# A fused attention and feed-forward kernel: its instructions issued in the main block of the program instead of in a block of their own

## The chip, the cores and the metric

The kernel runs on one core of a Trainium2 chip. The metric is the device time of one execution in microseconds (us), as the median over several runs. A core has five engines with an instruction stream each: TensorE (PE in the profile; its weight loads are PEld), VectorE (DVE), ScalarE (ACT), GpSimd (POOL) and SyncE (SP). They meet only over semaphores.

## The reference

The kernel computes attention in a sliding window of 32 positions to either side, for 8 batches of 8 heads, 576 positions and a head size of 64, and feeds the result, as 4608 tokens of 512 numbers, through two matrix products with a squared ReLU between them.

```python
scores = scale * np.matmul(q, k.transpose(0, 1, 3, 2))
mask = np.abs(pos[:, None] - pos[None, :]) <= window
scores = np.where(mask, scores, -1000000000.0)
...
attn = attn / (np.sum(attn, axis=-1, keepdims=True) + 1e-09)
out = np.matmul(attn, v)
...
h = x @ w_in            # (4608, 512) @ (512, 2048)
r = np.maximum(h, 0.0)
g = r * r
return (g @ w_out)      # (4608, 2048) @ (2048, 512)
```

## The kernel before

The attention goes through 24 groups of 192 queries (`NG`), three for each batch. For each group q and k are loaded, turned so that the head size lies on the partitions, multiplied (`scores`), put through the exponential and the mask, multiplied with v (`pv`), divided by the row sums and turned once more into `XT` (`xturn`). The feed-forward part follows some groups behind: `mm1` multiplies a stretch of `XT` with the first weights and squares the ReLU into `GT`, and `mm2` multiplies 128 tokens of `GT` with the second weights and stores 128 rows of the output. The last 128 tokens are cut into three pieces of columns (`mm2_last`, lines 766 to 779), so that eviction and store of the first pieces lie beside the matmuls of the later ones. ScalarE issues the stores of the first and third piece, SyncE that of the second.

No engine function issues instructions directly. Each step calls `rec`, which notes the engine, the function to call, what it reads and writes, an estimated duration and a key. `Prog.schedule` then simulates the engines and the DMA queues with these durations and sorts all operations by their planned start. `Prog.emit` goes through that one list, issues for each operation the waits that it needs (line 248) and then the operation itself, on its engine's queue.

The end of `Gen.build` is where this is put together. After `p.schedule()` a block of the language is entered (line 859), `p.emit()` issues every instruction of the kernel, and seven waits are issued on SyncE (line 863), one for each semaphore of the output stores (`o0` to `o3`, `oA`, `oB`, `oC`). Pairs of these waits are joined, so that four instructions of the trace carry line 863. Then the block is left, and what it issues on being left has line 859 in the trace. No body for a single engine is opened in the block; the engines are addressed as `nc.tensor`, `nc.scalar` and so on. Line 884 constructs the program object, before the kernel is called, and what the constructor issues has that line.

Of the kernel before, what the change touches and what calls it, by code (L numbers as in the profile page):

```python
# [270 lines left out]
class Gen:  # L271
# [511 lines left out]
    def build(self):  # L783
        p = self.p
        self.k1 = 0
        self.moe = None
        K = -100.0
        self.setup_idle()
        self.setup_iota(K + IOTA)
        self.setup_id(K)  # L790
        self.setup_mask(2, K + 1)
        self.setup_bias(2, K + 1.1)
        self.setup_mask(1, K + 2)
        self.setup_bias(1, K + 2.1)
        self.setup_k(0, K + 0.5)
        self.setup_v(0, K + 1.5)
        self.setup_v(1, VSET[0])
        self.setup_v(2, VSET[1])
        self.setup_mask(0, MKEY[0])
        self.setup_mask(3, MKEY[1])  # L800
        for i in range(3, NV):
            self.setup_v(i, -9)
        self.setup_k(1, -9)
        for n, it in enumerate(self.opening()):
            kd, a = it[0], it[1:]
            key = K + n
            if kd == "w1":
                self.load_w1(a[0], key)
            elif kd == "w2":
                self.load_w2(a[0], key)  # L810
            elif kd == "v":
                self.load_v(*divmod(a[0], 3), key, a[1:])
            elif kd[0] == "h":
                self.load_hw(kd[1], a[0], key)
            else:
                self.load_pair(kd, *divmod(a[0], 3), key)
        for g in (1, 2, 4, 5):
            self.copy_v(g, K + 7 if g < 3 else 3 * g - LEAD - AHEAD)
        todo = []

        def at(key, f, *a):
            todo.append((key, len(todo), f, a))

        for G in range(NG):
            b, g = divmod(G, 3)
            if b > 1:
                key = 3 * G - LEAD - AHEAD
                for t in "kq":
                    for c in PIECES[t][g]:
                        at(key, self.load_qk, t, b, c, key)  # L830
                at(key, self.load_v, b, g, key)
                if g and G < NVR:
                    key = 3 * G - LEAD - 0.5 if G >= VCS else key
                    at(key + 0.01, self.copy_v, G, key - VKEY if G >= VCS else key)
            for t in "kq":
                key = 3 * G - LEAD - (0.6 if b < NTURN else 3)
                for c in (g,) if b < NTURN else PIECES[t][g]:
                    at(key, self.turn_pe if b < NTURN else self.turn_dma, t, b, c, key)
            for ws in ((0,), (1,)) if G < NSPLIT else ((0, 1),):
                at(3 * G - LEAD + 0.3 * ws[0], self.scores, G, ws)  # L840
            for w in range(2):
                at(3 * G - LEAD + 0.3 * w + 0.1, self.pv, G, w)
            at(3 * G - LEAD + 0.5, self.xturn, G)
        t0 = 0
        while t0 < NTOK:
            n = FIRST[t0] if t0 in FIRST else 192 if t0 < 768 else 256 if t0 < T512 else 512
            m = min(512 // n, 4)
            for d in range(0, 16, m):
                key = t0 / 64 + d / 16 * n / 64
                at(key, self.mm1, t0, n, list(range(d, d + m)), key)  # L850
            t0 += n
        at(500, self.mm2_last, NBLK - 1, 500)
        for u in range(NBLK - 1):
            for seg in range(4):
                at(2 * u + LAG + seg * 0.5, self.mm2, u, seg, 2 * u + LAG + seg * 0.5)
        for key, _, f, a in sorted(todo, key=lambda x: x[:2]):
            f(*a)
        p.schedule()
        with self.nc.Block():
            dsems, dcount = p.emit()  # L860
            for s in dsems:
                if s[0] == "o":
                    self.nc.sync.wait_ge(dsems[s], dcount[s])
# [35 lines left out]
```

## Time and profile before

| what | before |
|---|---|
| time, median of 3 runs | 303.6 us |
| lowest and highest run | 303.34 and 303.64 us |
| span of the profiled execution, first to last instruction | 301.1 us |
| TensorE busy in the span | 291.9 us (97%) |
| instructions in the trace | 6232 |
| mean granted TensorE clock | 1.000 |

The profile is of one execution. Its span goes from the first to the last instruction of the program; the page shows no time of that execution beside the span, and the median of the runs is the nearest to it. Drains, waits and other instructions of an engine's sequencer are in the trace, with a small q behind the engine's name, but don't count as busy time. Views of one line list its instructions with the number of them, the least, median and longest duration in ns, and the first and last start in us from the span's start. The chain of waits is followed back from the last instruction that an engine, and not its sequencer, executed.

### The profile page before, as it was taken

The page shows a single profiled execution, that of the slowest core. Times are in us where ns is not written, and L with a number is a line of the kernel's source. Part 1 is how long each engine was busy: PE and PEld are TensorE (multiplying, and loading weights), DVE is VectorE, ACT ScalarE, POOL GpSimd, SP SyncE. Part 2 cuts the span into 40 slices and gives each one's busy share as a digit, 9 for nine tenths or more (in the row PEclk, how much of TensorE's full clock was granted, in tenths as well). Part 3 has the DMA queues.
Part 4 walks back from the last instruction along what each step waited for, and adds up shares of the span by engine and source line. Part 5 has one row for each costly group of instructions (what it writes and reads, how often), then busy time and mean ns, then how long its engine had stood idle before and what let it go on. Part 6 is the DMA issues. An engine that isn't in the chain of part 4 may idle for free.

```text
span 301.1 us, 6232 instructions
## 1 busy us (share of the span) xinstructions
PE 291.9 (97%) x2394; PEld 170.9 (57%) x2431; DVE 166.5 (55%) x385; ACT 160.7 (53%) x250; POOL 102.4 (34%) x131
## 2 busy tenths in 40 slices
PE   7899999999999999999999999999999999999996
PEld 2578866846677777764444445445444444444445
DVE  5898785726766766664378756666456322222100
ACT  3587834826567646644656666455636443443312
POOL 8993335406543543654065454330000000000000
PEclk9999999999999999999999999999999999999999
DMA  9999999999998999999999999994121201000112
GB/s 167 176 206 183 196 178 176 168 163 208 175 158 138 141 160 191 147 157 177 199 152 135 166 162 143 199 168 101 54 50 49 60 35 37 35 35 36 37 70 105
DMA packets 160060, 39.83 MB, mean 132 GB/s; under 512 B 149408, under 2 KB 155552, under 8 KB 160032
## 3 DMA queue, kind: packets, MB, share of 16 engines
q0 software_dynamic: 105824, 17.93, 86.1%
q1 hardware_dynamic: 48880, 12.14, 28.4%
q10 hardware_dynamic: 5328, 9.37, 8.9%
q8 instruction: 19, 0.31, 0.4%
q14 instruction: 9, 0.07, 0.1%
HBM read 36.70 MB, written 9.44 MB: 153 GB/s over the span
## 4 chain that ended last, share of the span: by engine, by line
PE 87%; DMA 7%; POOL 3%; issue 1%; ACT 1%; DVE 0%; ACTq 0%; POOLq 0%
PE ht L721 41%; PE outp L741 38%; DMA w<-in_moe_w_in_dram 5%; PE at L606 4%; PE at L548 3%; DMA xt<-xa 2%; POOL v L427 1%; POOL w L440 1%; PE at L469 1%; PE ht L766 1%; PE outp L766 1%; POOL kpair L410 1%; POOL qpair L410 1%; ACT rt L727 0%; ACT oe L751 0%
## 5 line engine op out<-in xcount | busy, mean ns | idle before, releaser
L721 PE MATMUL ht<-xt,w 128*128 128x256 bf16 (+2 forms) x886 | 142.4, 302 | 1.7 <-DMA xt<-xa 0.5
L741 PE MATMUL outp<-w,gt 128*128 128x512 bf16 x535 | 134.3, 379 | 1.4 <-issue 0.2
L727 ACT ACTIVATE rt<-ht 128x512 bf16<-128x512 f32 (+1 forms) x152 | 86.4, 577 | 90.8 <-PE ht L721 85.7
L721 PEld LDWEIGHTS ht<-xt,w 128*128 128x128 bf16 x896 | 80.8, 98 | 43.8 <-DMA xt<-xa 1.0
L730 DVE TENSOR_TENSOR gt<-rt 128x512 bf16<-128x512 bf16 (+1 forms) x152 | 61.3, 408 | 65.0 <-ACT rt L727 63.2
L741 PEld LDWEIGHTS outp<-w,gt 128*128 128x128 bf16 x560 | 52.3, 98 | 56.0 <-ACT oe L751 1.1
L378 POOL DMA_DIRECT2D kraw<-in_k_dram x30 | 25.3, 850 | 95.2 <-PE at L548 76.5
L573 ACT ACTIVATE e<-at 128x1024 bf16<-128x1024 f32 x46 | 44.8, 1021 | 11.2 <-PE at L548 11.1
L578 DVE TENSOR_TENSOR pt<-e,mask 128x1024 bf16<-128x1024 bf16 x46 | 31.5, 691 | 24.7 <-ACT e L573 24.6
L427 POOL DMA_DIRECT2D v<-in_v_dram x48 | 38.4, 822 | 0.0
L751 ACT ACTIVATE oe<-outp 128x512 f32<-128x512 f32 x35 | 21.1, 602 | 24.1 <-PE outp L741 24.1
L378 POOL DMA_DIRECT2D qraw<-in_q_dram x30 | 25.5, 860 | 0.0
L606 PEld LDWEIGHTS at<-v,pt 128*128 128x128 bf16 x384 | 18.0, 98 | 10.0 <-DVE at L634 1.8
L606 PE MATMUL at<-v,pt 128*128 128x65 bf16 x384 | 20.1, 194 | 0.5 <-ACT pt L570 0.5
L628 DVE TENSOR_TENSOR xb<-at,rs 128x512 bf16<-128x512 f32 x24 | 16.6, 690 | 1.1
L628 DVE TENSOR_TENSOR xa<-at,rs 64x512 bf16<-64x512 f32 x24 | 16.7, 695 | 0.8
L548 PEld LDWEIGHTS at<-qt,kt 64*128 64x128 bf16 x384 | 10.8, 94 | 8.3 <-issue 7.5
L548 PE MATMUL at<-qt,kt 64*128 64x128 bf16 x384 | 15.2, 217 | 0.1
L625 DVE RECIPROCAL rs<-at 64x8 f32<-64x8 f32 (+1 forms) x48 | 10.0, 209 | 9.5 <-PE at L606 7.8
L634 DVE MEMSET at<- 64x520 f32 x23 | 11.3, 492 | 3.7 <-DVE xa L628 2.9
L434 DVE COPY v<-v 64x512 bf16<-64x512 bf16 x16 | 5.8, 366 | 6.9 <-PE ht L721 5.8
L773 DVE COPY oe<-ht 128x128 f32<-128x128 f32 x1 | 0.3, 291 | 14.7 <-PE ht L766 14.7
(67 smaller groups left out, 82.1 us busy)
## 6 DMA issues: line engine op xcount, KB each, us to landing
out_dram<-oe ACTq DMA_DIRECT2D x35, 256.0 KB, 3.8
kraw<-in_k_dram POOLq DMA_DIRECT2D x24, 128.0 KB, 5.6
qraw<-in_q_dram POOLq DMA_DIRECT2D x24, 128.0 KB, 5.9
w<-in_moe_w_in_dram POOLq DMA_DIRECT2D x4, 512.0 KB, 10.6
v<-in_v_dram POOLq DMA_DIRECT2D x16, 128.0 KB, 7.3
w<-in_moe_w_out_dram POOLq DMA_DIRECT2D x4, 512.0 KB, 18.9
v<-in_v_dram POOLq DMA_DIRECT2D x16, 96.0 KB, 6.7
v<-in_v_dram POOLq DMA_DIRECT2D x16, 64.0 KB, 5.8
```

Source lines behind the costliest of these rows:

```text
L378: self.p.rec("POOL", lambda e: e.dma_start(raw[0:n, x % 2, :].rearrange("p (h d) -> p h d", h=8), s), writes=[("raw", t, x // 2, x % 2)], ...
L427: self.p.rec("POOL", lambda e, j=j, lo=lo, hi=hi, k0=k0: e.dma_start(vt[lo - k0:hi - k0, j, :, 0:64], self.v[b, :, lo:hi, :].rearrange("h ...
L548: mm = e.matmul(sc[:, 512 * par + 128 * j:512 * par + 128 * j + 128], kt[r:r + 64, j, k0:k0 + 128], q, start=G >= NBIAS, stop=True, skip_g ...
L573: self.p.rec("ACT", lambda e, e_=e_, sc=sc: e.activation(e_[:], sc, ACTF.Exp, scale=0.125), reads=tags[w], writes=[("e", n % 2)], key=key, ...
L578: self.p.rec("DVE", lambda e, pt=pt, ee=ee, mb=mb: e.tensor_tensor(pt[:], ee, mb, ALU.mult), reads=[("e", n % 2), ("mask", mi)], writes=[( ...
L606: mm = e.matmul(avp[:, c:c + 65], pt[:, 4 * (h % 2) + h // 2, :], vt[:, w, h, 0:65], start=(w == 0 and y == 0), stop=True, skip_group_chec ...
L628: self.p.rec("DVE", lambda e: e.tensor_tensor(x[r0:128, :].rearrange("p (x y c) -> p x y c", x=2, y=4), av[:, :, :, 0:64], rb, ALU.mult), ...
L721: mm = e.matmul(ht[:, n * x:n * x + n], self.W1[:, ft, 128 * d:128 * d + 128], self.XT[:, ft, r:r + n], start=(ft == 0), stop=(ft == 3))
L727: self.p.rec("ACT", lambda e: e.activation(rt[:, 0:c], ht[:, 0:c], ACTF.Relu), reads=[f"ht{k % 2}"], writes=[("rt", k % 4)], key=key, dur= ...
L730: self.p.rec("DVE", lambda e: e.tensor_tensor(gt[:, d0:d0 + len(ds), r:r + n], rr, rr, ALU.mult), reads=[("rt", k % 4)], writes=[("gt", s, ...
L741: mm = e.matmul(op[:], gt[:, d, r:r + 128], self.W2[:, d, :], start=(d == 0), stop=(d == 15))
L751: self.p.rec("ACT", lambda e: e.activation(oe, op[:], ACTF.Copy), reads=[f"outp{u % 2}"], writes=[("oe", u % 4)], key=key, dur=act(512), n ...
```

## The change

The block is no longer entered. `p.emit()` and the waits for the stores stand under a condition that is always true, with the same indentation, so that they are issued in the block that is open when the kernel is called, the program's main block. Nothing else of the kernel is different.

```diff
@@ -856,7 +856,7 @@
         for key, _, f, a in sorted(todo, key=lambda x: x[:2]):
             f(*a)
         p.schedule()
-        with self.nc.Block():
+        if True:
             dsems, dcount = p.emit()
             for s in dsems:
                 if s[0] == "o":
```

## The prediction

> **What bounds the kernel now.** I read the page of the profiled execution first, then the view of everything issued from the line of the block, the waits of SyncE, and the first and last microseconds. The page:
>
> ```profile
> span 301.1 us, 6232 instructions
> PE 291.9 (97%) x2394; PEld 170.9 (57%) x2431; DVE 166.5 (55%) x385; ACT 160.7 (53%) x250; POOL 102.4 (34%) x131
> ...
> PE 87%; DMA 7%; POOL 3%; issue 1%; ACT 1%; DVE 0%; ACTq 0%; POOLq 0%
> ```
>
> TensorE is busy for 97% of the span and makes up 87% of the chain of waits. A change that leaves the order and the waits of the matmuls alone can touch only what lies ahead of the first matmul, behind the last one, or outside the span. So the two ends are what has to be read. The last microseconds, in the order of time:
>
> ```profile
> 297.82 0.94 PE L766 MATMUL ht<-w,gt 128*128 128x128 bf16 x14
> 297.92 0.29 DVE L773 COPY oe<-ht 128x128 f32<-128x128 f32 x1 [14.66 <-PE ht L766]
> ...
> 298.23 0.38 SPq L779 DMA_DIRECT2D out_dram<-oe  x1
> 298.87 0.28 ACT L776 ACTIVATE oe<-ht 128x128 f32<-128x128 f32 x1 [1.46 <-PE ht L766]
> 299.18 0.34 ACTq L779 DMA_DIRECT2D out_dram<-oe  x1
> ```
>
> Behind the last matmul (297.82 + 0.94 = 298.76) come one eviction on ScalarE and the last store, issued at 299.18. Its transfer takes this long, and SyncE waits for it at line 863:
>
> ```profile
> DMA to landing us min/median/max: 1.6/1.7/1.7
> ...
> L863 SPq EVENT_SEMAPHORE  x4: 17/28/28, 298.7 to 300.8; - x4
> ```
>
> 299.18 + 1.7 is 300.9, and the last of SyncE's four waits stands at 300.8, so it is the landing of the last store that ends it. The span ends at 301.1. The rest is what the block issues when it is closed:
>
> ```profile
> L859 POOLq EVENT_SEMAPHORE  x2: 17/17/17, 300.9 to 301.0; - x2
> L859 POOLq DRAIN  x1: 7294/7294/7294, 197.2 to 197.2; - x1
> L859 PEldq DRAIN  x1: 1195/1195/1195, 297.6 to 297.6; - x1
> L859 DVEq DRAIN  x1: 328/328/328, 297.9 to 297.9; - x1
> L859 ACTq DRAIN  x1: 153/153/153, 299.6 to 299.6; - x1
> L859 SPq DRAIN  x1: 13/13/13, 300.9 to 300.9; - x1
> L859 SPq EVENT_SEMAPHORE  x1: 17/17/17, 301.1 to 301.1; - x1
> L859 ACTq EVENT_SEMAPHORE  x1: 17/17/17, 301.1 to 301.1; - x1
> L859 DVEq EVENT_SEMAPHORE  x1: 21/21/21, 301.1 to 301.1; - x1
> L859 PEldq EVENT_SEMAPHORE  x1: 51/51/51, 301.1 to 301.1; - x1
> ```
>
> These are all the instructions that line 859 has in the trace: five drains and six semaphore instructions, 11 in all, with first start 197.2 and last start 301.1. Not one of them stands at the beginning, and none is a branch. It is a barrier: each engine drains and reports, GpSimd collects the reports and releases the others, and each passes when released. Entering the block costs nothing here; only closing it does.
>
> **The change, part by part.** *What stays at the beginning.* There is a barrier of the same make in the first microsecond, from line 884, which constructs the program object, and which the diff doesn't touch:
>
> ```profile
> L884 POOLq EVENT_SEMAPHORE  x2: 17/17/17, 0.5 to 0.6; - x2
> L884 SPq DRAIN  x1: 7/7/7, 0.0 to 0.0; - x1
> ...
> L884 PEldq EVENT_SEMAPHORE  x1: 51/51/51, 0.7 to 0.7; - x1
> ```
>
> The first transfers, matmuls and weight loads start behind that one, and go on starting behind it. Nothing at the front is removed, added or moved: 0.
>
> *What stays in the middle.* The work of all queues is sorted by the planner before the block is entered, and each instruction is issued in that order with its own waits, with or without a block. The block opens no body for a single engine. So SyncE's loads and transposes, GpSimd's loads and ScalarE's stores keep their places: 0, and if I am wrong here, TensorE's 291.9 us will say so.
>
> *What goes at the end.* The four drains of GpSimd, TensorE, VectorE and ScalarE lie beside other work. The longest, GpSimd's 7.294 us, begins at 197.2 and is over at 204.5, some 96 us ahead of the end. TensorE's is over at 297.6 + 1.2 = 298.8, VectorE's at 297.9 + 0.3 = 298.2, ScalarE's at 299.6 + 0.15 = 299.75. All lie under the flight of the last store, which lands at 300.8. Removing them gains nothing; without that cover they would cost up to 1.2 us (TensorE's). What is not covered is all that follows SyncE's last wait: its drain of 13 ns, the collecting and releasing on GpSimd (2 x 17 ns and the ways between), and the passing of the released engines, TensorE's 51 ns as the longest. SyncE's own time in it has a row, the only wait of line 859 there:
>
> ```profile
> SPq L863 <- DMA out_dram<-oe: 2.0, 3, 0.8
> SPq L859 <- PEq L859: 0.2, 1, 0.2
> ```
>
> So the uncovered part is 0.013 + 0.2 + 0.051 = 0.26 us. The rounding of the two ends bounds it: the last wait ends between 300.78 and 300.88 (300.75 to 300.85, and 28 ns), and the span between 301.05 and 301.15, which leaves 0.17 to 0.37. For the collecting half there is the barrier at the beginning, in the chain of waits:
>
> ```profile
> 0.56 0.06 issue
> 0.62 0.02 POOLq L884
> 0.64 0.11 issue
> 0.75 0.01 POOLq L316
> ```
>
> From 0.56 to 0.75 it is 0.19 us, without a drain before it and the 51 ns behind it; together 0.25. I take 0.26.
>
> *What takes its place.* Nothing of the kernel's own is late next: SyncE's four waits for the stores stay, so the program still ends with the last landing. Four engines now run off the end of their streams early, by rows above at 204.5 or before (GpSimd), 298.2, 298.8 and 299.75, instead of all at 301.1. What the chip does with them then has no row: the trace holds the kernel's instructions alone. The page gives no time for the profiled execution beside its span. The runs' median of 303.6 is 2.5 us above the span, and these 2.5 us hold everything ahead of the first and behind the last instruction, profiling differences included. So the unknown term is bounded by -2.5 (all of it is done early) and, on the other side, by the dearest drain of an engine that still has work, +1.2 less the 0.26. Of its values I take 0: SyncE, the engine that is last in both kernels, still has its whole way through the ending ahead of it.
>
> The sum: 301.1 - 0.26 = 300.84 for the span, and 303.6 - 0.26 = 303.34 for the time, or 303.3.
>
> There is one page that bears on the unknown term: in the Trainium skill, "Runtime: NRT & Kernel Launch", section "The ~15µs preamble/postamble breakdown" says that after the kernel the runtime places a barrier of its own in which all engines are waited for, and that clearing the semaphores comes only behind it. By that rule the early engines can't begin the ending, so the gain stays at the barrier's own time, 0.26; its figures for that ending, about 1.5 us for the barrier and about 1.5 for the clearing, add to more than the 2.5 us that lie outside the span here, and the rule's order is not visible in this trace.
>
> **The rivals.** *The ending shrinks too.* If each engine has something of its own to do at the end of a program before it meets the others, four of five now do it under the flight of the last store, and only SyncE's part is left. For it: GpSimd, VectorE, TensorE and ScalarE are free at least 1.0 us before 300.8. Against it: SyncE is last as before, and if the parts are done side by side and are of one length, the gain is nil. The price: take half of the 2.5 us as lying behind the span, 1.25, and half of that as saved, 0.6. Then 303.34 - 0.6 = 302.7.
>
> *The barrier is hidden anyway.* Another meeting of the engines follows at once, and the one that goes had already lined them up; its time is then spent in the next one. For it: the barrier at the beginning takes the same 0.25 us, so engines that have to be lined up pay about this whoever asks for it. Against it: a second meeting needs its own time behind the first one, so both are in the time of before. Time 303.6.
>
> *Slower: the emptying of the engines comes at the end.* The drains stand now where they cost nothing, each behind its engine's last work. If an engine is instead emptied by what follows the program, and only after SyncE's last wait, a drain comes onto the path. It decides when it exceeds the 0.26 us that went. For it: GpSimd's drain took 7.294 us at its place and TensorE's 1.195, so they are not always short. Against it: both had work in flight when they began; SyncE's drain at 300.9, with nothing in flight, took 13 ns, and by 300.8 every engine is in that state. At TensorE's price the time is 303.34 + 1.2 = 304.5.
>
> *The change doesn't do what it says.* If a barrier is issued at the end of every program anyway, the 11 instructions come back under another line. For it: one is issued at the beginning without being asked for (line 884). Against it: that one belongs to the constructor. Time 303.6, as for the hidden barrier.
>
> **How the numbers follow.** Forecast 0.54 at 303.3, with a range of its own of 303.0 to 303.6, since the three runs of before lie 0.3 us apart (303.34 to 303.64); the shrinking ending 0.30 at 302.7; hidden anyway or not done, together 0.09 at 303.6; slower 0.07 at 304.5. The predicted time is the likeliest, 303.3. Down to 302.6 the range takes in more than half of the shrinking ending, and up to 303.7 all of the hidden barrier; what is left out is the rest of the one and the slower case, under 0.2. What a measurement can tell from no change is about 0.2%, 0.6 us: faster means below 303.0, slower above 304.2. The forecast puts 0.06 below 303.0 and the rest within; the shrinking ending 0.28 below and 0.02 within; the cases at 303.6 put 0.08 within and 0.01 above. That is 0.34 faster, 0.58 within, and 0.08 slower.
>
> **What would show it.** No drain and no semaphore instruction from line 859, and 6232 - 11 = 6221 instructions. The last instruction of the trace is SyncE's fourth wait at line 863, and the span is 300.8 to 300.9. Line 884 has the same rows, and TensorE is busy for 291.9 us within a few tenths. If the span falls by 0.26 but the time falls by more than 0.6, the ending shrinks. If the span falls and the time doesn't, the barrier was hidden. If TensorE's busy time or its first matmul moves by more than a few tenths, then the block did something to the stream that this trace doesn't show, and my reading of line 859 is wrong.

## The result, and the profile after

The changed kernel took 302.39 us (median of 10 runs, 301.48 to 303.15); the kernel before, run beside it and counted with its three earlier runs, took 303.3 us (10 runs, 303.06 to 304.06). The ratio is 0.9966, with a 95% interval of 0.9953 to 0.998: faster by 0.9 us. The prediction was 303.3, in a range of 302.6 to 303.7; the measured time lies below the range.

First the page of the changed kernel, then its view of what line 863 issues (instructions, least, median and longest ns, first and last start), then its answer for line 859:

```profile
span 301.5 us, 6221 instructions
...
PE 292.0 (97%) x2394; PEld 171.4 (57%) x2431; DVE 166.6 (55%) x385; ACT 160.7 (53%) x250; POOL 102.6 (34%) x131
```

```profile
L863 SPq EVENT_SEMAPHORE  x4: 17/28/28, 299.4 to 301.5; - x4
```

```profile
nothing on L859; most used: ['L721', 'L741', 'L548', 'L606', 'L248', 'L469', 'L727', 'L730', 'L766', 'L378', 'L509', 'L313', 'L427', 'L625', 'L628', 'L573', 'L578', 'L751', 'L753', 'L634', 'L701', 'L704', 'L884', 'L434', 'L597']
```

The 11 instructions are gone, TensorE is as busy as before, and the program ends with SyncE's last wait. So far it is as forecast. But this execution's span is longer than the one shown of before (301.5 against 301.1), though a barrier is missing from it, and its time is shorter. Each run of the changed kernel has its own time and span, and they answer the second half of this: 302.86 and 301.5, 301.48 and 300.2, 303.15 and 301.8. **Time less span** is 1.28 to 1.36 us in all ten, with a mean of 1.33. Before the change only one span was known, and no time of the same execution.

Where the span went is in the timelines of TensorE, before and after (start, duration, and in brackets the idle time before):

```profile
69.33 1.05 PE L721 MATMUL ht<-xt,w 128*128 128x256 bf16 x8 [0.53 <-DMA xt<-xa]
```

```profile
70.14 1.03 PE L721 MATMUL ht<-xt,w 128*128 128x256 bf16 x8 [1.12 <-issue]
```

These are the only waits of TensorE in its timelines between 60 and 90 us. The same matmul waited 0.6 us longer in the execution shown of after. What it waits for is a turned tile of the attention's result, which SyncE sends for with line 701; the profile names this releaser before, and none after ("issue"). The views of that one transfer, before and after, show that it was issued at about the same time and took 0.8 us longer to land, at about 69.2 and 70.1 us, each time just ahead of the matmul:

```profile
L701 SPq DMA_TRANSPOSE xt<-xa x1: 1267/1267/1267, 62.0 to 62.0; - x1
...
DMA to landing us min/median/max: 7.2/7.2/7.2
```

```profile
L701 SPq DMA_TRANSPOSE xt<-xa x1: 1272/1272/1272, 62.1 to 62.1; - x1
...
DMA to landing us min/median/max: 8.0/8.0/8.0
```

So this part of the difference lies 230 us ahead of the end of the program. The end itself:

```profile
299.54 0.28 ACT L776 ACTIVATE oe<-ht 128x128 f32<-128x128 f32 x1 [1.40 <-PE ht L766]
299.84 0.34 ACTq L779 DMA_DIRECT2D out_dram<-oe  x1
```

From the issue of the last store (299.84) to the end of the span it is 1.7 us; before it was 1.9 (299.18 to 301.1), so the barrier's quarter of a microsecond did go.

### The profile page after: what moved, and what is told of

It is laid out like the page before. It is cut to its first block, busy times and chain, and to the rows that moved or that the text cites. A ratio compares the mean times of both kernels' runs of the same rounds, so it can differ in the third digit from the quotient of the medians.

```text
span 301.5 us, 6221 instructions
## 1 busy us (share of the span) xinstructions
PE 292.0 (97%) x2394; PEld 171.4 (57%) x2431; DVE 166.6 (55%) x385; ACT 160.7 (53%) x250; POOL 102.6 (34%) x131
## 4 chain that ended last, share of the span: by engine, by line
PE 90%; DMA 5%; POOL 3%; issue 1%; ACT 1%; POOLq 0%; ACTq 0%
PE ht L721 41%; PE outp L741 40%; DMA w<-in_moe_w_in_dram 5%; PE at L606 4%; PE at L548 3%; POOL v L427 1%; POOL w L440 1%; PE at L469 1%; PE ht L766 1%; PE outp L766 1%; POOL kpair L410 1%; POOL qpair L410 1%; ACT rt L727 0%; ACT oe L751 0%; ACT oe L776 0%
```

## The experiments

Two views were held against each other. *Theory E*: the ending of the program, outside the span, got shorter, because it no longer begins on all engines at once. *Rivals*: the ending is the same, and only the wandering span made the difference (S); or the drains, and not the lateness of the engines, make the ending long (D). What tells them apart is time less span, taken run by run: it also holds what lies ahead of the first instruction, so only differences of it are read. Between runs of one kernel it varied by about 0.1 us, at most by 0.2, while times and spans wander by some 2 us and more. All kernels but the one that changes the slack run the same operations in the same order; the order of the waits of one operation is not fixed by the source, and spans are known to 0.1 us, so span differences below that are not read.

**The kernel before, unchanged.**

> The kernel before, unchanged, to have time and span of the same execution. Theory E (the ending shrinks): time less span is 2.2 to 2.5 us in every run, against the 1.33 us of the changed kernel, and the spans lie between 300.7 and 301.7. Rival S (the ending is the same and only the stream ran differently): time less span is 1.3 us here too, and the spans lie near 302.

Time less span was 2.15 us on average (2.11 to 2.18); over the runs of before beside it, 31 in number, 2.13. That is a little below what theory E expected (2.2 to 2.5) and far from S, which falls: against the changed kernel's 1.33, 0.80 of the gain lies outside the span.

**The changed kernel, built anew.**

> The changed kernel once more, built anew. Theory E: time less span is 1.28 to 1.36 us again, whatever the span. Rival S: the difference of 0.9 us to the kernel before doesn't come back; ratio 0.998 to 1.002.

302.3 us against 303.45, ratio 0.9953 (0.9933 to 0.9973), and time less span 1.32. The gain came back.

**The four other engines held until SyncE is done.** The edit, in the changed kernel:

```diff
-                    self.nc.sync.wait_ge(dsems[s], dcount[s])
+                    last = self.nc.sync.wait_ge(dsems[s], dcount[s])
+            end = self.nc.alloc_semaphore("s_end")
+            last.then_inc(end, 1)
+            for e in (self.nc.tensor, self.nc.vector, self.nc.scalar, self.nc.gpsimd,):
+                e.wait_ge(end, 1)
```

> Without the block, but SyncE's last wait raises a semaphore for which TensorE, VectorE, ScalarE and GpSimd wait as their last instruction; no drains, no collecting. Theory E: the four engines end late again, so time less span goes back to 2.2 to 2.5 us, and the time is only 0.1 to 0.2 below that of the kernel before. Rival D (the drains or the collecting on GpSimd made the ending long): time less span stays at 1.3 us and the time is that of the changed kernel plus 0.1.

Time less span was 1.81 (1.77 to 1.87), between what the two theories said: of the 0.80 us, 0.49 come from the engines' lateness alone (1.81 against 1.32), without drains and collecting. The time itself is unclear (ratio 0.9997, 0.9963 to 1.0031), for the spans of these runs wandered most: two of the ten were 304.2 and 304.6 us long, both with a mean granted TensorE clock of 0.994, and eight lay between 300.4 and 302.4 at 1.000.

**The drains alone.**

```diff
+            for e in (self.nc.tensor, self.nc.vector, self.nc.scalar, self.nc.gpsimd, self.nc.sync):
+                e.drain()
```

> Without the block, but every engine issues its drain behind its last instruction, with no semaphore. Theory E: as the changed kernel, time less span 1.3 us, ratio to the kernel before 0.9966 within 0.002. Rival D: time less span is 2.2 to 2.5 us and the time is that of the kernel before, less at most 0.2.

1.30, and a ratio of 0.9956 (0.9937 to 0.9975): as the changed kernel. The view of the line has all five drains; the two longest took about as long as before (7294 and 1195 ns there):

```profile
L865 POOLq DRAIN  x1: 7356/7356/7356, 197.1 to 197.1; - x1
L865 PEldq DRAIN  x1: 1195/1195/1195, 297.5 to 297.5; - x1
```

So drains cost nothing here where no engine has to meet another behind them.

**Each of the other engines last.** In the changed kernel the waits for the output stores stand on another engine:

```diff
-                    self.nc.sync.wait_ge(dsems[s], dcount[s])
+                    self.nc.gpsimd.wait_ge(dsems[s], dcount[s])
```

> As the changed kernel, but the waits for the output stores stand on TensorE, so that TensorE ends last and SyncE ends with its last store. Theory P (every engine has a closing part of its own length, and the latest end decides): time less span is TensorE's own closing time, 1.3 to 1.8 us, and among TensorE, VectorE, ScalarE and GpSimd at least one has 1.7 to 1.8, as with all of them held. Theory Q (the closing parts are alike and get in each other's way when several engines end together): 1.3 us within 0.1, as with SyncE last.

> The waits for the output stores on VectorE. Theory P: time less span is VectorE's own closing time, anywhere from 1.0 to 1.8 us. Theory Q: 1.3 us within 0.1.

> The waits for the output stores on ScalarE, behind its own last store. Theory P: ScalarE's own closing time, anywhere from 1.0 to 1.8 us. Theory Q: 1.3 us within 0.1.

> The waits for the output stores on GpSimd, which has no other work after 205 us. Theory P: GpSimd's own closing time, and if one engine made the 1.8 us it is most likely this one. Theory Q: 1.3 us within 0.1.

| engine that ends last | time less span, mean (range) | ratio to before (interval) |
|---|---|---|
| SyncE (the changed kernel) | 1.33 (1.28 to 1.36) | 0.9966 (0.9953 to 0.998) |
| ScalarE | 1.47 (1.43 to 1.52) | 0.9965 (0.9947 to 0.9982) |
| TensorE | 1.56 (1.53 to 1.59) | 0.9974 (0.9959 to 0.999) |
| VectorE | 1.62 (1.50 to 1.68) | 0.9983 (0.9957 to 1.001) |
| GpSimd | 2.10 (2.07 to 2.14) | 1.0005 (0.9987 to 1.0022) |

The rows of line 863 with TensorE last, and with GpSimd last, show that each is the last instruction of its trace, at the spans 300.4 and 300.7:

```profile
L863 PEldq EVENT_SEMAPHORE  x4: 51/51/51, 297.1 to 300.3; - x4
```

```profile
L863 POOLq EVENT_SEMAPHORE  x4: 17/43/43, 289.2 to 300.6; - x4
```

What theory P forecast holds, and Q falls: the time outside the span depends on which engine is last, from SyncE's 1.33 to GpSimd's 2.10. With GpSimd last, and no barrier anywhere at the end, the time is that of the kernel before. What the engines do there is in no trace. A closing part of each engine's own, as P has it, is argued; an ending that goes through the engines one behind the other in a fixed order could give differences between them too, and no run tests that.

**One engine or a crowd.** GpSimd alone held by SyncE's last wait, and then the other three without it:

> As the changed kernel, but GpSimd alone waits, as its last instruction, for the semaphore that SyncE's last wait raises. Theory P1 (GpSimd's own closing decides, and it is shorter behind a single wait than behind several): time less span is 1.8 us, as with all four engines held. Theory C (GpSimd's closing is short behind a single wait, and the 1.8 us came from a crowd of five that end together): 1.3 to 1.5 us.

> TensorE, VectorE and ScalarE wait for the semaphore of SyncE's last wait, GpSimd doesn't. Theory P1: the longest of the three closing times measured with each engine last, 1.47, 1.56 and 1.62, less what the engine ends ahead of the others: 1.55 to 1.62 us. Theory C: 1.7 to 1.8 us.

```profile
L867 POOLq EVENT_SEMAPHORE  x1: 17/17/17, 300.6 to 300.6; - x1
```

With GpSimd alone it is 1.83 (1.80 to 1.88), as with all four; with the three others 1.60 (1.57 to 1.64), which is what the slower of them have alone. Nothing is added by their number. The late end of GpSimd accounts for the whole 0.49.

**How much GpSimd has behind the landing.** 1.83 is less than the 2.10 with GpSimd last and the 2.13 with the barrier. The next runs have a barrier without drains, in place of the block; two and four waiting instructions on GpSimd in place of one; and the block of before without GpSimd's drain. Two waits are joined into one instruction, so the edit for two instructions issues four waits and that for four issues eight:

```diff
+            self.nc.all_engine_barrier(sem_only=True)
```

```diff
-        with self.nc.Block():
+        with self.nc.Block(no_gpsimd_drain=True):
```

> In the main block, closed by a barrier of the language that only collects and releases over semaphores, with no drains. Theory P1: GpSimd has two instructions behind the last landing and is as late as in the kernel before, so time less span is 2.1 us and the time is that of the kernel before within 0.1. Rival D (the drains take part): time less span is 1.8 us or less.

> As the run that holds GpSimd alone, but with two waiting instructions on GpSimd in place of one. Theory P1: 2.1 us, that is 0.3 more than with one. If the number of instructions doesn't matter: the same as with one.

> GpSimd alone held, with four waiting instructions behind SyncE's last wait. Theory P1 (each instruction of GpSimd behind the landing adds to its ending): with 1.83 us for one and 1.98 for two, 2.2 to 2.4 us for four. Rival (one step from one to more than one, then flat): 2.0 to 2.1 us.

> The kernel before with the block told to leave out GpSimd's drain alone; the other four drains, the collecting and the releasing stay. If GpSimd's drain is a part of what its ending is long by: time less span 1.94 us, as with the barrier without any drains, against 2.13 with all of them. If another engine's drain makes that difference: 2.13 us.

| on GpSimd, behind the last landing | time less span, mean (range) |
|---|---|
| one waiting instruction, a single wait | 1.83 (1.80 to 1.88) |
| two waiting instructions, each of two waits | 1.98 (1.93 to 2.10) |
| four waiting instructions, each of two waits | 2.08 (2.05 to 2.10) |
| GpSimd last, from above: one waiting instruction of two waits | 2.10 (2.07 to 2.14) |
| barrier without drains: collect and release | 1.94 (1.87 to 2.08) |
| block without GpSimd's drain: collect and release | 1.96 (1.89 to 2.04) |
| block as before: its drain, collect and release | 2.13 (2.08 to 2.20) |

GpSimd's rows for the two barriers without its drain show the two instructions:

```profile
L864 POOLq EVENT_SEMAPHORE  x2: 17/17/17, 301.4 to 301.4; - x2
```

```profile
L859 POOLq EVENT_SEMAPHORE  x2: 17/17/17, 301.6 to 301.7; - x2
```

Of the expectations, the one for two instructions was too high (2.1) and that for four too (2.2 to 2.4): the second adds 0.15, two further ones 0.1 together, as the rival had it (2.0 to 2.1). The barrier without drains came between its two (2.1, and 1.8 or less).

The number of instructions behind the landing is not what decides, though. The run with GpSimd last has only one there, as its view from 300 us on shows, and 2.10 all the same:

```profile
L863 POOLq EVENT_SEMAPHORE  x1: 43/43/43, 300.6 to 300.6; - x1
```

That instruction is a joined wait of 43 ns, and so are those of the runs with two and four, while the one of 1.83 was a single wait of 17 ns:

```profile
L867 POOLq EVENT_SEMAPHORE  x2: 43/43/43, 300.8 to 300.9; - x2
```

```profile
L867 POOLq EVENT_SEMAPHORE  x4: 43/43/43, 301.0 to 301.2; - x4
```

So number and form changed together. With GpSimd last, two more waits also ended within the last 2 us, ahead of the landing; whether these count, or the form does, no run separates.

Leaving out GpSimd's drain takes 0.17 off outside the span, though the drain itself was over some 96 us earlier. That edit has a side effect: the other four engines then report with instructions of their own, so that line 859 has 14 instructions in place of 11. On GpSimd only the drain is missing. The barrier without any drain has such reports too and comes to about the same, 1.94, so the other four drains add next to nothing. Why GpSimd's ending is longer or shorter by these tenths is open.

**More instructions on SyncE.**

> The changed kernel with two more waiting instructions on SyncE behind its last wait. Theory P1, if it holds for SyncE as for GpSimd: time less span 1.33 + 0.15 to 1.33 + 0.3 us. If only GpSimd's ending grows with its instructions: 1.3 us within 0.05, and the span grows by 0.1 to 0.2.

1.30 (1.27 to 1.33) and a ratio of 0.9957 (0.994 to 0.9973): what lengthened GpSimd's ending, two joined waits, doesn't lengthen SyncE's.

**The wander of the span.** One constant of the changed kernel: `XSLACK = 4500` in place of 2500.

> The changed kernel with the planner told that the transposed tiles of the attention's result land 2 us later (XSLACK 4500 for 2500), which moves TensorE's work around the wait at 70 us and behind it. Theory W (the executions differ by TensorE's wait for the transposed tile near 70 us): the spans lie closer together, within 0.7 us for most, near 300.3, and the time is 301.6 to 302.0. Rival: the wander comes from elsewhere and the spans still spread over 1.5 us.

TensorE's waits between 20 and 302 us in this run are these alone:

```profile
PE at L606 <- DVE at L634: 0.5, 2, 0.2
PE ht L721 <- DMA w<-in_moe_w_in_dram: 0.3, 1, 0.3
```

The wait of 1.12 us near 70 us is gone, and nine of ten spans lie between 300.9 and 301.6, against 300.2 to 302.2 for the 20 runs of the changed kernel; the tenth was 304.9, at a mean granted clock of 0.994. The planner paid for it elsewhere, though: the lowest span is 300.9 and not 300.2, and 302.5 us, above the 301.6 to 302.0 that were expected, with a ratio of 0.9975 (0.9945 to 1.0005), is no better than the changed kernel. Since the constant moves the whole order of work, this run alone doesn't show what the wait is worth. Other traces, all at a clock of 1.000, agree about it. In the second run of the changed kernel, with a span of 301.6, TensorE waited this long between 60 and 80 us:

```profile
PE ht L721 <- DMA xt<-xa: 1.1, 1, 1.1
```

With VectorE last, in a span of 302.2, it was 1.2 us. With GpSimd alone held (300.6), with TensorE last (300.4) and with the two further waits on SyncE (300.5) there was no wait of TensorE in that stretch. So the wait for the turned tile makes about 1 us of the wander. The rest is not accounted for: the run with four waiting instructions on GpSimd had no such wait either, and a span of 301.3, of which these four take 0.3. No run showed a version that is clearly faster than the changed kernel; the one with the added drains, the one with the two further waits on SyncE and the one with ScalarE last are equal to it within their intervals.

## Why the prediction was right or wrong

*Right: what the block issues.* Line 859 stood for the closing barrier alone; 6221 instructions, line 884 and TensorE's 292.0 us are as said, and the last instruction is SyncE's fourth wait.

*Right: the span's share.* 0.26 us, with bounds of 0.17 to 0.37. The distance from the issue of the last store to the end fell from 1.9 to 1.7 us, and the mean spans of 114 runs of before, those beside the experiments, and of 20 of after are 301.36 and 301.05. The 0.3 between them agrees with 0.26, though the wander makes it a weak witness. That the span shown of after would be 300.8 to 300.9 was wrong: I took the rest of the span as fixed from one execution, and a wait near 70 us moves it by a microsecond.

*Wrong: the unknown term.* The step that failed is "Of its values I take 0: SyncE, the engine that is last in both kernels, still has its whole way through the ending ahead of it". The premise is right, the conclusion isn't, for SyncE's way is the shortest of the five: with GpSimd last the time outside the span is 2.10, with SyncE last 1.33. In the kernel before, GpSimd came through the barrier at about the same time as SyncE (its last row starts at 301.0, SyncE's at 301.1), and the 2.13 there must be GpSimd's, since none of the other four came to more than 1.62 when it was last. The term is -0.80, and the steps to it are measured: 0.50 from a GpSimd that is held by one wait (1.83 against 1.33), 0.13 more with a collect and release in its place (1.96), 0.17 more with its drain (2.13). Why the last two steps cost what they do is open. With 0.26 in the span the sum is 1.06; 0.91 and 1.15 were measured in the two comparisons, and the wander of the spans is larger than their difference.

*The rival that won.* "The ending shrinks too" had the mechanism and a price of 0.6 by halving twice, which gave 302.7; the measured term of 0.80 makes it 303.34 - 0.8 = 302.5 from the same start. The start was high as well: the three runs had a median of 303.6, ten runs 303.3. The rival had 0.30 of the chance. The argument held against it was that parts "done side by side and of one length" save nothing. Four late engines cost no more than GpSimd alone (1.81 and 1.83), which fits the first half; the runs with each engine last refute the second.

*The rule of the Trainium skill.* By "Runtime: NRT & Kernel Launch", section "The ~15µs preamble/postamble breakdown", the runtime's barrier behind the kernel comes ahead of the clearing, and I concluded that early engines could begin nothing. The runs contradict the conclusion: an engine that is free early does save time, 0.50 us where GpSimd is no longer held. So not all of the ending waits for the last engine. Whether the engines meet in the barrier of that rule, no run here shows.

*The others.* The slower case fell: drains were over long before, and with no drains at all or with all five the changed kernel has the same 1.3. The barrier was not hidden by another, and none came back under another line.

## What to carry to other kernels

A barrier at the end of a program can cost more than the tenths that it shows in the trace, here 0.26 us in it and 0.80 outside: it makes every engine end late, and the engine with the longest ending then sets the time. Let each engine run out when its work is over, and put the last wait on the engine with the shortest ending, SyncE here; GpSimd, with the longest, should be done early. And take the time and the span of the same execution before arguing about what lies between them: one pair from the kernel before would have shown nothing wrong, but a second kernel's pair shows at once whether the change is inside the span or outside.

## What the hardware showed that was not expected

The ending depends on the engine that is last: time less span was 1.33, 1.47, 1.56, 1.62 and 2.10 us for SyncE, ScalarE, TensorE, VectorE and GpSimd. Late engines don't add up: four cost no more than GpSimd alone (1.81 and 1.83). GpSimd's ending also depends on what it executes at the end (1.83 for one single wait, 1.98 and 2.08 for two and four joined ones, 2.10 for one joined wait behind the landing and two shortly ahead of it), SyncE's doesn't (1.33, and 1.30 with two joined waits more). And a drain of GpSimd that was over 96 us before the end went with an ending that was 0.17 us longer.
